# Chunked attention feeding a top-1 mixture of experts: the order in which a pair's keys, queries and values are asked for

## The chip, the cores and the metric

One core of a Trainium2 chip runs the whole program. The metric is device time in microseconds (us) of one execution, as the median of the runs shown.

## The reference, cut to what matters

```python
B, H, S, D = 4, 8, 768, 64          # batch, heads, sequence, head size
chunk, left_ctx, right_ctx = 32, 16, 8
for c in range(S // chunk):          # 24 chunks
    q_c   = q[:, :, 32*c : 32*c+32]
    k_ctx = k[:, :, max(0, 32*c-16) : min(S, 32*c+40)]     # v_ctx likewise
    scores = scale * q_c @ concat(mem_k, k_ctx).T          # 8 memory keys in front
    a = softmax(scores)
    out[:, :, 32*c : 32*c+32] = a @ concat(mem_v, v_ctx)
x = out as (3072 tokens, 512)
e = argmax(x @ w_gate + modality_bias[modality_id])        # one of 8 experts per token
y[token] = gate * (relu(x @ w1[e]) @ w2[e])                # 512 -> 1024 -> 512
```

## The kernel before, in words

The attention works on 16 **pairs** of heads, numbered u = 0 to 15 (two heads of one batch entry, 128 columns together). Each pair has two halves (hf = 0 and 1) of 12 chunks, and the main loop goes over these 32 units, written `(u, hf)`. The order on every engine is the order of the program text: nothing is rearranged by a planner, so an instruction that waits holds up all that stands behind it on its engine or queue. In the turn of one unit the loop computes the scores of that unit (`scores`, L329), the transposed exponentials of the unit before it (`trans_p`, L346), the product with the values of the unit before it (`attend`, L358), and the transpose of the normalized result of the unit before that (`trans_x`, L383). Beside it the loop prepares the next pairs.

Three kinds of transfer bring a pair's inputs in, all issued on SyncE's queue (SP):

- `load_qk(u)` (L94) asks for the keys and then the queries of pair u, one DMA each, into tiles of a pool with three buffers. The keys' buffer comes free when the keys of pair u - 3 have been transposed (`trans_k`, L311), the queries' buffer when the queries of pair u - 3 have been regrouped (`regroup_q`, L278, on VectorE).
- `load_v(u)` (L255 to L257) asks for the values of pair u with six DMAs into one of three window tiles. It has to wait until `attend` of the second half of pair u - 3 has read that tile.
- `load_mv(u)` (L264) copies the memory values into the same tile with two DMAs.

From pair 6 on the keys of pair u + 2 are half transposed in unit (u, 1) and the other half in unit (u + 1, 0), and `regroup_q(u + 2)` runs in unit (u, 1). GpSimd (POOL) spreads the values of pair u + 1 to the overlapping windows in unit (u, 1): `share_v`, two copies at L268, which wait for the values to land. Behind them on POOL stand, in order, the store of pair u - 1's result (`store_x`, L376), for some pairs a store of gates (L623), the memory keys of pair u + 2 (`mem_keys`, L303), which `scores(u + 2, 0)` needs, and for every fourth pair POOL's share of the routing's one-hot matrices (L657, L660), which the matmuls at L668 read.

After four pairs the tokens of one batch entry are complete, and `route` picks their experts in small steps between the attention's. The expert matmuls follow the attention; the weights of the first expert are asked for once three of the four batch entries have been routed.

The end of the turn of unit (u, 0), for u from 1, issues the loads: values and memory values of pair u + 2 (`NVW` is 3), then keys and queries of pair u + 4. `NU` is 16.

Of the kernel before, what the change touches and what calls it, by code (L numbers as in the profile page):

```python
# [45 lines left out]
def tile_chunk_attention_top1_moe(  # L46
# [16 lines left out]
    NU = B * H // 2  # L63
# [25 lines left out]
    def load_qk(u):  # L89
        r0 = u * 2 * S  # L90
        q2s[u] = ld.tile([P, 6, 2 * D], F32, name="q2")
        k2s[u] = ld.tile([P, 6, 2 * D], F32, name="k2")
        for t, f in ((k2s[u], kf), (q2s[u], qf)):
            nc.sync.dma_start(t.rearrange("p (h i) e -> p h (i e)", h=2), f[r0:r0 + 2 * S].rearrange("(h p j) d -> p h (j d)", h=2, p=P))  # L94
# [153 lines left out]
    def load_v(u):  # L248
        vw = vws[u % NVW]
        for h in range(2):  # L250
            hh = 2 * u + h
            r0 = 64 * h

            src = bass.AP(tensor=vf.tensor, offset=(hh * S + 8) * D, ap=[[D, 32], [32 * D, NCH - 1], [1, D]])
            nc.sync.dma_start(vw[r0 + 24:r0 + 56, h, 0:NCH - 1, 0:D], src)  # L255
            nc.sync.dma_start(vw[r0 + 24:r0 + 48, h, NCH - 1, 0:D], vf[hh * S + S - 24:hh * S + S])
            nc.sync.dma_start(vw[r0 + 16:r0 + 24, h, 0, 0:D], vf[hh * S:hh * S + 8])  # L257

    def load_mv(u):
        vw = vws[u % NVW]  # L260
        for h in range(2):
            hh = 2 * u + h
            r0 = 64 * h
            nc.sync.dma_start(vw[r0 + 56:r0 + 64, h].rearrange("p c d -> p (c d)"), mvx[hh // 16][8 * (hh % 16):8 * (hh % 16) + 8].rearrange("p c d -> p (c d)"))  # L264
# [691 lines left out]
    for i in range(n + 2):  # L956
        live = i < n
        u, hf = units[i] if live else (NU, i % 2)
# [124 lines left out]
        if i < 2:  # L1083
            load_qk(i + 3)
        if live and hf == 0 and u >= 1:
            if u - 1 + NVW < NU:
                load_v(u - 1 + NVW)
                load_mv(u - 1 + NVW)
            if u + 4 < NU:
                load_qk(u + 4)  # L1090
        if i == 5:
            small_loads()
# [251 lines left out]
```

## Time and profile before

| | |
|---|---|
| median of 3 runs | 424.61 us |
| the three runs | 423.15, 424.61 and 427.23 us |
| the profiled execution, its own time | 421.46 us |
| its span, from the first to the last instruction | 419.7 us |
| mean granted TensorE clock | 0.997 of full speed |
| TensorE busy (PE) | 402.2 us, 96% of the span |
| VectorE (DVE), ScalarE (ACT), GpSimd (POOL) busy | 338.8, 301.4 and 238.8 us |
| DMA packets | 82543, of which 50659 are under 512 bytes |

The rows below come from the profiled execution. Times are microseconds from the start of the span. The span is 1.76 us shorter than that execution's time, and that execution was 3.15 us faster than the median of the three runs. The attention takes the first 130 us or so of the span. A busy TensorE isn't TensorE at its peak, since matmuls are pipelined and their ends are modelled.

### The profile page before, as it was taken

What the parts mean: (1) busy time and instruction counts of PE and PEld (TensorE: products, weight loads), DVE (VectorE), ACT (ScalarE), POOL (GpSimd) and SP (SyncE); (2) the same over time, 40 slices, a digit from 0 to 9 for tenths busy, and PEclk for the clock granted to TensorE, in tenths of its full rate; (3) what the DMA queues carried; (4) which work ended last, traced back from release to release, by engine and by line L of the source; (5) the groups of instructions that cost most, each with busy time, mean ns of one, the idle gap of its engine ahead of it and who ended that gap; (6) DMA issues with size and microseconds to landing.
All of it is one profiled execution on the core that took longest, in us unless ns stands there. A gap on an engine that the chain in (4) does not pass through costs nothing.

```text
span 419.7 us, 11402 instructions
## 1 busy us (share of the span) xinstructions
PE 402.2 (96%) x3875; PEld 340.6 (81%) x3875; DVE 338.8 (81%) x788; ACT 301.4 (72%) x594; POOL 238.8 (57%) x320
## 2 busy tenths in 40 slices
PE   7999998998999999999999999999999999999993
PEld 4777896787867989899998888888888888888882
DVE  7889697798897889769979887788989688988750
ACT  7777886796765557467566887868778678878750
POOL 8986678778681619776753654463866076520101
PEclk9999999999999999999999999999999999999998
DMA  9899899999859600334423769969757232410101
GB/s 218 183 271 237 196 256 184 282 238 198 197 160 261 214 15 2 102 103 76 102 76 61 274 207 266 316 165 357 211 209 232 78 79 79 91 61 2 51 3 56
DMA packets 82543, 66.81 MB, mean 159 GB/s; under 512 B 50659, under 2 KB 71339, under 8 KB 82476
## 3 DMA queue, kind: packets, MB, share of 16 engines
q1 hardware_dynamic: 75276, 46.36, 44.7%
q0 software_dynamic: 6784, 19.50, 15.0%
q8 instruction: 33, 0.54, 0.6%
q14 instruction: 34, 0.28, 0.2%
q10 hardware_dynamic: 416, 0.13, 0.1%
HBM read 84.64 MB, written 12.76 MB: 232 GB/s over the span
## 4 chain that ended last, share of the span: by engine, by line
PE 63%; issue 13%; DMA 10%; POOL 6%; DVE 5%; ACT 1%; POOLq 1%; SPq 0%; ACTq 0%; DVEq 0%
PE av L843 12%; PE tr L831 11%; PE sc L843 10%; PE tr L812 9%; PE tr L815 5%; PE av L358 3%; DMA vw<-in_v_dram 3%; DMA q<-in_q_dram 2%; PE sc L329 2%; DMA k<-in_k_dram 2%; DMA out_dram<-o,ix_now 1%; PE tr L383 1%; PE tr L346 1%; PE tr L311 1%; POOL vw L268 1%
## 5 line engine op out<-in xcount | busy, mean ns | idle before, releaser
L743 DVE TENSOR_TENSOR w<-raw,w 128x512 fp32r<-128x512 f32 x96 | 68.0, 752 | 3.9 <-ACT w L742 3.6
L812 PE MATMUL tr<-xt,w 128*128 128x512 f32 x256 | 70.1, 395 | 0.0
L843 PE MATMUL av<-wh,h 128*128 128x512 f32 x192 | 61.5, 393 | 0.0
L268 POOL COPY vw<-vw 24x1472 f32<-24x1472 f32 x31 | 44.4, 1431 | 19.2 <-DMA vw<-in_v_dram 18.0
L742 ACT CAST w<-raw 128x512 fp32r<-128x512 f32 x96 | 53.9, 622 | 1.5 <-DMA raw<-in_moe_w_dram 1.5
L843 PE MATMUL sc<-wh,h 128*128 128x512 f32 x160 | 50.8, 392 | 0.0
L812 PEld LDWEIGHTS tr<-xt,w 128*128 128x128 f32 x256 | 44.3, 189 | 7.2 <-DVE wl L824 0.8
L831 PE MATMUL tr<-xt,w 128*128 128x256 f32 x384 | 48.1, 284 | 0.7 <-DVE xt L807 0.7
L831 PEld LDWEIGHTS tr<-xt,w 128*128 128x128 f32 x384 | 46.8, 191 | 2.0 <-DVE xt L807 0.9
L321 ACT COPY kbd<-tr 64x672 f32<-64x672 f32 x57 | 44.8, 786 | 3.1 <-PE tr L315 1.9
L815 PEld LDWEIGHTS tr<-xt,w 128*128 128x128 f32 x256 | 39.2, 189 | 5.4
L843 PEld LDWEIGHTS av<-wh,h 128*128 128x128 f32 x192 | 36.0, 188 | 7.5 <-issue 0.2
L848 POOL DMA_INDIRECT out_dram<-o,ix_now x22 | 25.6, 1162 | 28.7 <-ACT o L847 23.0
L815 PE MATMUL tr<-xt,w 128*128 128x256 f32 x256 | 40.7, 281 | 0.0
L821 DVE TENSOR_TENSOR hs<-tr,hs 128x256 f32<-128x256 f32 x64 | 26.8, 419 | 13.3 <-ACT hs L818 13.2
L843 PE MATMUL av<-wl,h 128*128 128x512 f32 x96 | 37.5, 390 | 0.0
L752 POOL DMA_INDIRECT xg<-gd,gx x24 | 27.8, 1156 | 14.8 <-DMA gd<-gt 9.2
L822 ACT ACTIVATE h<-hs 128x256 fp32r<-128x256 f32 x64 | 26.8, 418 | 12.0 <-DVE hs L821 10.3
L843 PEld LDWEIGHTS sc<-wh,h 128*128 128x128 f32 x160 | 30.0, 188 | 6.4 <-issue 0.2
L824 DVE TENSOR_TENSOR wl<-vw,wh 128x512 fp32r<-128x512 f32 x48 | 33.3, 694 | 2.3
L825 DVE SCALAR_TENSOR_TENSOR h<-hs,h 128x256 fp32r<-128x256 f32 x64 | 28.3, 442 | 7.7 <-ACT h L822 7.7
L752 POOL DMA_INDIRECT xg<-xd,gx x24 | 27.8, 1157 | 8.7 <-issue 4.8
(266 smaller groups left out, 902.8 us busy)
## 6 DMA issues: line engine op xcount, KB each, us to landing
raw<-in_moe_w_dram SPq DMA_DIRECT2D x96, 256.0 KB
vw<-in_moe_w_dram SPq DMA_DIRECT2D x72, 256.0 KB
k<-in_k_dram SPq DMA_DIRECT2D x16, 384.0 KB
q<-in_q_dram SPq DMA_DIRECT2D x16, 384.0 KB
xd<-xb POOLq DMA_DIRECT2D x16, 384.0 KB, 5.2
kbd<-in_moe_w_dram SPq DMA_DIRECT2D x24, 256.0 KB
vw<-in_v_dram SPq DMA_DIRECT2D x32, 184.0 KB
xall<-in_moe_w_dram SPq DMA_DIRECT2D x4, 1024.0 KB
```

What stands on the lines that cost most here:

```text
L268: copy(vw[r0:r0 + 24, h, 1:NCH, 0:D], vw[r0 + 32:r0 + 56, h, 0:NCH - 1, 0:D])
L321: copy(dst.rearrange("p c (i j) -> p c i j", j=2)[:, :, :, j], win)
L742: nc.scalar.copy(wh[i], raw[i])
L743: (eng or nc.vector).tensor_sub(wl[i], raw[i], wh[i].bitcast(F32))
L752: nc.gpsimd.indirect_dma_start(out=xg[t][:, part], out_offset=None, in_=rows, in_offset=bass.IndirectOffsetOnAxis(ap=gx[:, t:t + 1], axis=0))
L812: nc.tensor.matmul(ph, wh[f][:, c * P:(c + 1) * P], xt[:, c].rearrange("p a n -> p (a n)"), start=(c == 0), stop=False, skip_group_check=True)
L815: nc.tensor.matmul(ph[:, 0:256], wl[f][:, c * P:(c + 1) * P], xth[:, c], start=False, stop=(c == 3), skip_group_check=True)
L821: nc.vector.tensor_add(hs, ph[:, 0:256], hs)
L824: nc.vector.tensor_sub(wl[w], raw[w], wh[w].bitcast(F32))
L825: nc.vector.scalar_tensor_tensor(hl[:, f], hs, 0.0, hh[:, f].bitcast(F32), op0=ALU.max, op1=ALU.subtract)
L831: nc.tensor.matmul(ph, w[f][:, c * P:(c + 1) * P], x[:, c, :], start=(n == 0), stop=(n == 11))
L843: nc.tensor.matmul(pos[t], x, w[8 + f], start=(f == 0 and n == 0), stop=(f == 7 and n == 2))
```

## The change

```diff
         if live and hf == 0 and u >= 1:
+            if 3 <= u < NU - 4:
+                load_qk(u + 4)
             if u - 1 + NVW < NU:
                 load_v(u - 1 + NVW)
                 load_mv(u - 1 + NVW)
-            if u + 4 < NU:
+            if u < 3:
                 load_qk(u + 4)
```

In the nine turns u = 3 to 11 the two DMAs of `load_qk(u + 4)` now stand in front of the eight DMAs of `load_v(u + 2)` and `load_mv(u + 2)` on SP, where they stood behind them. The turns u = 1 and 2 keep the old order, and from u = 12 on there are no keys left to ask for. No instruction is added or taken away, and no other engine's order changes.

## Rows read from the trace of the kernel before

**Rows 1.** Busy time by stretch: us, five engines (instructions), clock, DMA share, GB/s.
```profile
50.00:60.00 10.00, 10.00 (x199) 8.93 (x198) 8.45 (x28) 8.62 (x17) 5.68 (x6) 1.00 1.04 239
```

**Rows 2.** Waits of the engines, 30 to 115 us: total, times, longest.
```profile
POOL vw L268 <- DMA vw<-in_v_dram: 17.1, 10, 3.1
...
DVE qr L278 <- DMA q<-in_q_dram: 2.5, 4, 1.6
...
PE tr L311 <- DMA k<-in_k_dram: 1.1, 1, 1.1
```

**Rows 3.** Waits of SP's queue, 40 to 110 us.
```profile
SPq L264 <- DMA q<-in_q_dram: 7.2, 7, 1.6
```

**Rows 4.** Chain that ended last, in order of time: start, length, what.
```profile
59.45 5.69 DMA vw<-in_v_dram
...
65.16 6.47 DMA k<-in_k_dram
```

**Rows 5.** PE by time: start, length, line, operation, idle time before and its releaser.
```profile
60.34 0.87 PE L358 MATMUL av<-vw,PT 128*32 128x130 f32 x24
...
63.43 0.87 PE L358 MATMUL av<-vw,PT 128*32 128x130 f32 x24
64.12 0.84 PE L329 MATMUL sc<-kbd,qT 128*32 128x128 f32 x24
...
67.17 1.23 PE L668 MATMUL tr<-a,l 128*128 128x192 f32 x6
68.33 0.88 PE L358 MATMUL av<-vw,PT 128*32 128x130 f32 x24
...
71.76 0.52 PE L311 MATMUL tr<-ident,k 128*128 128x128 f32 x3 [1.10 <-DMA k<-in_k_dram]
...
72.72 0.87 PE L358 MATMUL av<-vw,PT 128*32 128x130 f32 x24
...
75.45 0.27 PE L311 MATMUL tr<-ident,k 128*128 128x128 f32 x1 [0.51 <-issue]
...
76.48 0.87 PE L358 MATMUL av<-vw,PT 128*32 128x130 f32 x24
```

**Rows 6.** SP's queue by time: the issues around three pairs.
```profile
52.91 0.40 SPq L255 DMA_DIRECT2D vw<-in_v_dram  x1
...
58.44 0.39 SPq L94 DMA_DIRECT2D k<-in_k_dram  x1
58.94 0.40 SPq L94 DMA_DIRECT2D q<-in_q_dram  x1
59.45 0.40 SPq L255 DMA_DIRECT2D vw<-in_v_dram  x1
...
65.16 0.39 SPq L94 DMA_DIRECT2D k<-in_k_dram  x1
```

**Rows 7.** PE by time: the transpose that frees a keys' buffer.
```profile
52.66 0.49 PE L311 MATMUL tr<-ident,k 128*128 128x128 f32 x3
```

**Rows 8.** DMA issues by line, KB each.
```profile
k<-in_k_dram SPq DMA_DIRECT2D x16, 384.0 KB
q<-in_q_dram SPq DMA_DIRECT2D x16, 384.0 KB
```

**Rows 9.** Busy time by stretch, as in Rows 1, in shorter stretches.
```profile
44.00:46.00 2.00, 2.00 (x31) 1.64 (x27) 1.97 (x6) 1.95 (x4) 1.64 (x2) 1.00 0.37 47
...
60.00:62.00 2.00, 2.00 (x54) 1.64 (x53) 1.90 (x9) 1.96 (x4) 1.99 (x2) 1.00 1.00 350
62.00:64.00 2.00, 2.00 (x34) 1.83 (x36) 1.97 (x5) 1.92 (x6) 1.79 (x5) 1.00 1.33 209
66.00:69.00 3.00, 2.44 (x36) 1.83 (x38) 2.86 (x7) 2.40 (x5) 2.94 (x3) 1.00 0.66 73
```

**Rows 10.** POOL by time: values shared, memory keys, one-hot matrices.
```profile
58.54 2.88 POOL L268 COPY vw<-vw 24x1472 f32<-24x1472 f32 x2 [2.23 <-DMA vw<-in_v_dram]
...
63.06 0.73 POOL L303 COPY kbd<-memT 64x192 f32<-64x192 f32 x2
...
66.53 1.01 POOL L660 TENSOR_SCALAR a<-iota,ac,tokm 128x192 fp32r<-128x192 f32 x1
67.61 2.87 POOL L268 COPY vw<-vw 24x1472 f32<-24x1472 f32 x2
```

## The prediction

> **What bounds the kernel now.** I read the profile from coarse to fine: busy time by stretch, then who waited for whom, then the chain that ended last, then the queue and the two engines around the places that the chain names. In a stretch of the attention's middle TensorE's records cover all of the 10 us and the DMA engines' mean share is 1.04, at 239 GB/s [rows 1]. So both the attention's own work and the transfers are close to their limit, and neither has much to give. The waits say which of them is late. By far the longest is POOL's, 17.1 us in ten places, for values to land; VectorE waits 2.5 us for queries and TensorE itself only 1.1 us, once, for keys [rows 2]. The reader should not take the longest for the costliest: POOL's wait costs only where somebody waits for POOL.
>
> Where somebody does is seen in TensorE's own steps. The product with the values opens each turn's last part. From 60.34 to 63.43 two of them are 3.09 us apart, with no idle time of note between them; that is the step when nothing is late. The one at 72.72 comes 4.39 us after that at 68.33, so 1.30 us late, and the transpose at 71.76 shows why: 1.10 us of idle time, ended by keys that landed [rows 5]. These are the keys of pair 10. The chain goes through the same place: keys asked for at 65.16, 6.47 us until they were there, and their issue itself came right after values asked for at 59.45 had taken 5.69 us [rows 4]. SP doesn't run ahead freely; its issues of the memory values waited 7.2 us in seven places for queries asked for earlier [rows 3]. The queue moves at the pace at which transfers land.
>
> All other late steps that I can name (routing matmuls, VectorE and ScalarE between two of them) have nothing to do with the order of the loads. So what the change can win is small against 424.61 us: the 1.30 us, and what the queries' waits cost.
>
> **What moves, and its price.** The change adds and removes nothing. Per turn it moves two DMAs, keys and queries, past eight on the same queue; no other queue is passed. Their issues take 0.39 and 0.40 us [rows 6]; 58.44 to 59.45 is the two with what lies between, 1.01 us, and that is what SP does earlier. The data is 2 x 384 KB [rows 8], 786 thousand bytes; at the 350 GB/s of the stretch in which such transfers ran [rows 9] that is 2.25 us of all DMA engines.
>
> Since the loads form a cycle (keys and queries, values, memory values), swapping them in nine consecutive turns is one shift: in turn 3 one set of keys and queries is put in, in turns 4 to 11 the cycle is the old one with keys one pair further ahead, and at turn 12 one set is missing. So keys come about one turn earlier, and values at most one set later, once, not nine times.
>
> *The keys' side.* Pair 10's keys take the place that pair 9's had, 58.44 in place of 65.16 [rows 6]: 6.72 us earlier against a lateness of 1.30 us. Could they be held up there by their buffer? It comes free with the transpose that ends at 53.15 [rows 7], 5.3 us sooner, so the values behind them aren't held up by it either. The stretch from 66 to 69, in which DMA moved only 73 GB/s [rows 9], then meets pair 11's keys, which have a turn to spare. I count the whole 1.30 us as won. The queries of pair 10 kept VectorE idle for 1.6 us [rows 2], and the step after it, 72.72 to 76.48, is 0.67 us too long; but 0.51 us of that is idle time at 75.45 which the row puts down to "issue" [rows 5], to no landing. So 0 to 0.67 us; I take 0.2, near the rest of 0.16, because the row names another reason for most of it.
>
> *The values' side.* From turn 3 on they stand behind one set more. Upper bound: the set's 2.25 us. Lower bound: the inserted set (pair 7's) is issued near 40 us and moves in a stretch where the engines have room; from 44 to 46 they moved 47 GB/s [rows 9], which is 1.7 us of 2 unused at 350 GB/s. That leaves 0.5 us. If the stretch up to 46 has more room than that, the shift is nothing, and if the queue no longer runs dry there, even some tenths below. I take 0.5, since the row that is nearest in time to the insertion says so; the range keeps 2.25.
>
> Who pays for 0.5 us? POOL spreads pair 7's values from 58.54, having waited 2.23 us for them, and behind that stand two stores, then the memory keys of pair 8, which end at 63.79 [rows 10]. The scores of pair 8 start at 64.12 [rows 5]: 0.33 us of room, the tightest place that I found. A shift of 0.5 us makes them 0.17 us late. Behind the memory keys POOL makes one-hot matrices until 67.54 [rows 10], and the routing matmuls run from 67.17 to 68.40 [rows 5], so the last of them has been waiting on POOL already and takes the full 0.5. These are the same delay seen twice, not two: 0.3 us between them. Then the next values are spread from 67.61 with no wait of POOL's before them [rows 10], so a shift up to about that size is absorbed there.
>
> What hides the rest: the longer waits of POOL in other turns have a turn's slack behind them, and by then TensorE waits for neither. If that cover were gone, each 1 us of shift would be 1 us at most per place.
>
> The sum: -1.30 - 0.2 + 0.3 = -1.2 us. Whatever the attention wins reaches the end, because the first expert's work starts from the last pairs. Against the profiled execution's own time, 421.46 us (span 419.7), this gives 420.3; that execution was 3.15 us faster than the median of the three runs, so for the median I take 424.61 - 1.2 = 423.4 us.
>
> **A rule weighed against the trace.** After the keys' issue at 58.44 and the values' at 59.45 [rows 6] the stretch 60 to 62 runs at 350 GB/s and the stretch 62 to 64 at 209 [rows 9], as if large packets went first and small ones after. The Trainium skill, page "DMA: Bandwidth & Descriptors", section "Queues, rings and completion order", says that each DMA engine takes the descriptors of one ring in their order; by that, what is put in front delays what stands behind by its full length, and the shift would be 2.25 us. The trace agrees on the order; it doesn't say that no gap absorbs the length. What a full shift would cost is the third rival's sum, which is made from rows.
>
> **The rivals.**
>
> *Nothing comes of it (424.6 us).* The 1.30 us at 72.72 may be an accident of this execution: one wait of 1.1 us in one place, and the other queries late by 0.3 us on average (below). If the routing's POOL work is the true limit between 63 and 74, the step at 76.48 takes over and the gain of 1.5 us goes to it. For it: only one of nine turns shows a late key. Against it: the chain passes through that very key.
>
> *SP's issuing is the bound (424.6 us).* From 58.44 to 65.16 one cycle of ten issues fills 6.72 us of the queue [rows 6]. If that is the time that ten issues take, order is without effect: keys come earlier, something else comes later by as much, and every turn is as long as before. For it: hardly a gap in that cycle. Against it: SP waits for landings inside it [rows 3], so issue follows data. The Trainium skill, page "Perfetto Trace Analysis", section "What "DMA-bound" means", names a solid track of the issuing sequencer as a bound of its own, and by it this rival would hold; the trace shows the solid track, and the waits speak against the conclusion.
>
> *Values become the bound (slower: 426.2 us).* Mechanism: the set put in front in turn 3 isn't absorbed, pair 7's values land 2.25 us later, POOL's memory keys for pair 8 are late by 2.25 - 0.33 = 1.92 us, and TensorE waits at 64.12. It decides from a shift of 0.33 + 1.5 = 1.83 us on, where the loss passes the gain. Once gives -1.5 + 1.92 = +0.4; if the second routing stretch, with the same POOL work behind the same wait, pays again, 1.92 more, so +2.3, and I put the case between, at +1.6. For it: POOL's 17.1 us of waits show that values land last in most turns. Against it: the 47 GB/s just where the set goes in.
>
> *More is won (422.1 us).* If all waits on queries cost their time (2.5 us on VectorE) beside the 1.30 and nothing is paid for the values: -3.8 at most, -2.6 if half of the queries' is hidden. For it: VectorE is 85% busy [rows 1], so its idle time isn't all spare. Against it: queries' waits other than the longest average (2.5 - 1.6) / 3 = 0.3 us.
>
> That the loads don't come earlier at all (SP held at the keys' buffer) is excluded for pair 10 by the 5.3 us above.
>
> **How the numbers follow.** Forecast (between -2 and -0.4 us) 0.48, nothing 0.19, SP's issuing 0.08, slower 0.14, more 0.11. The three runs lie 4.1 us apart, so a shift under 1%, 4.2 us, can hardly be told from none with them. All five cases lie inside 1%; only their tails and the spread of the runs reach beyond. So faster 0.06, same 0.89, slower 0.05. The range takes in "more" and "slower" with about 1 us for the median's own scatter at the low end and half of that at the high end: 420.8 to 426.7 us.
>
> **What the profile after would show.** Right: the transpose of pair 10's keys without idle time for a landing, and keys asked for one turn earlier on SP; VectorE's waits for queries near nothing; POOL's waits for values as long as before or longer by half a microsecond each. The values' step is wrong if the scores after the memory keys, or the routing matmuls, show idle time ended by POOL, or if the first attention product of a pair waits for POOL's copies. The prediction as a whole fails if the attention ends more than 3 us earlier or later than before, which would mean that the order of loads decides more turns than the one that I found.

## The result, and the profile after

The median went from 423.17 us (420.98 to 427.23) to 425.93 us (423.71 to 429.78), 22 runs of each: a ratio of 1.0054 [1.0033, 1.0074], so slower by some 2.3 us (0.0054 of 423.17) where 1.2 us faster was forecast, and within 1% of before. Ratios and intervals go by fast runs alone: runs over 1.5% above the fastest of their kernel are left out, none of these 44 and, further down, one of the keys alone, two of the same with the memory keys in front and one of the last run of experiment 5. The profiled execution after has a span of 423.5 us, 3.8 more than that of before, at the same mean clock of 0.997; through the attention the granted clock was 1.00 in both.

The loss is made in the attention's middle. First TensorE by time, after, the same columns as in [rows 5]:

```profile
45.44 0.87 PE L358 MATMUL av<-vw,PT 128*32 128x130 f32 x24
...
51.27 0.86 PE L358 MATMUL av<-vw,PT 128*32 128x130 f32 x22 [0.47 <-POOL vw L268]
52.88 0.86 PE L329 MATMUL sc<-kbd,qT 128*32 128x128 f32 x24 [0.74 <-POOL kbd L303]
...
60.02 0.86 PE L329 MATMUL sc<-kbd,qT 128*32 128x128 f32 x24 [0.54 <-POOL kbd L303]
...
67.83 0.86 PE L329 MATMUL sc<-kbd,qT 128*32 128x128 f32 x24 [1.42 <-POOL kbd L303]
...
71.17 0.80 PE L668 MATMUL tr<-a,l 128*128 128x192 f32 x5 [0.76 <-POOL a L660]
71.91 0.87 PE L358 MATMUL av<-vw,PT 128*32 128x130 f32 x24
...
75.00 0.87 PE L358 MATMUL av<-vw,PT 128*32 128x130 f32 x24
...
78.21 0.27 PE L311 MATMUL tr<-ident,k 128*128 128x128 f32 x1 [0.66 <-issue]
...
121.28 0.87 PE L358 MATMUL av<-vw,PT 128*32 128x130 f32 x24
```

And the same view of before, at three points that the earlier rows don't show:

```profile
45.86 0.87 PE L358 MATMUL av<-vw,PT 128*32 128x130 f32 x24
...
51.51 0.84 PE L329 MATMUL sc<-kbd,qT 128*32 128x128 f32 x24
...
118.28 0.87 PE L358 MATMUL av<-vw,PT 128*32 128x130 f32 x24
```

Put the two side by side as "after minus before". The product with the values at 45.44 is still 0.42 us early. The scores of pair 6 are 1.37 late (52.88 against 51.51), those of pair 7 are at 60.02, and those of pair 8 are 3.71 late (67.83 against 64.12 in [rows 5]). At the next product the lateness is 3.58 (71.91 against 68.33), and then it falls to 2.28 (75.00 against 72.72): that fall of 1.30 us is the late key of [rows 5], which is gone. From there the lateness wanders to 3.00 at 121.28. So the gain came as forecast in this pair of executions, and about 4 us were lost ahead of it, 3.2 of them (0.47 + 0.74 + 0.54 + 1.42) in idle time of TensorE that POOL ended. The 0.76 us at 71.17 are POOL's too, but the lateness doesn't grow across them (3.71 ahead, 3.58 behind): the same routing matmuls were drawn out in the kernel before [rows 5].

The waits of the engines after, 30 to 118 us, columns as in [rows 2]:

```profile
POOL vw L268 <- DMA vw<-in_v_dram: 21.9, 8, 5.0
...
PEld sc L329 <- POOL kbd L303: 3.9, 4, 1.7
...
PE sc L329 <- POOL kbd L303: 2.7, 3, 1.4
...
PE tr L668 <- POOL a L660: 0.8, 1, 0.8
...
PE av L358 <- POOL vw L268: 0.5, 1, 0.5
```

The lines on keys and queries that landed late in [rows 2] have no counterpart in this list at all. New are TensorE's waits for POOL: 2.7 us for memory keys, 0.8 for one-hot matrices, 0.5 for spread values, 4.0 together against 1.1 for keys before. POOL's own wait for values went from 17.1 to 21.9 us.

Now POOL by time, after (columns as in [rows 10]), and under it the same of before:

```profile
47.97 3.25 POOL L268 COPY vw<-vw 24x1472 f32<-24x1472 f32 x2 [4.99 <-DMA vw<-in_v_dram]
51.17 0.88 POOL L376 DMA_DIRECT2D xd<-xb  x1
52.09 0.73 POOL L303 COPY kbd<-memT 64x192 f32<-64x192 f32 x2
...
67.04 0.73 POOL L303 COPY kbd<-memT 64x192 f32<-64x192 f32 x2
```

```profile
44.30 2.88 POOL L268 COPY vw<-vw 24x1472 f32<-24x1472 f32 x2 [0.98 <-DMA vw<-in_v_dram]
...
48.06 0.73 POOL L303 COPY kbd<-memT 64x192 f32<-64x192 f32 x2
```

Pair 5's values, the first that stand behind the set put in front, are spread from 47.97 in place of 44.30, 3.67 us later. The memory keys of pair 6 stand behind that on POOL and are done at 52.82 in place of 48.79. Before, that left 2.7 us until the scores at 51.51; after, the scores start 0.06 us behind them. The chain of waits of this stretch goes through the same steps, in order of time:

```profile
41.94 5.98 DMA vw<-in_v_dram
...
47.97 1.29 POOL vw L268
...
51.22 0.83 POOL xd L376
...
52.48 0.35 POOL kbd L303
...
52.88 0.86 PE sc L329 x24
```

One more execution of each kernel was profiled, with no edit, to see whether this is one execution's accident. Of before:

> The kernel before, a second profiled execution. Theory of the prediction (pair 10's keys are late by the order of the loads): TensorE waits for keys again at the same transpose, 0.7 to 1.5 us, and the step there is over 4.2 us. Rival (the 1.30 us were an accident of that one execution; the two profiled kernels in the old order that followed show no wait for keys): no wait for keys over 0.3 us, and the attention is 1 to 2 us shorter from pair 4 to pair 14 than in the first profile.

Of after:

> The changed kernel, a second profiled execution. Theory (late values through POOL): pair 5's values are spread from 47 to 49 us, scores wait for POOL's memory keys in at least three places, 2 to 4 us in all, and from pair 4 to pair 14 the attention is 2.5 to 4.5 us longer than in the second execution of the kernel before. Rival (collisions of VectorE's small steps with POOL's copies, which fall out differently each time, make the difference): scores' waits for POOL under 1 us and the excess in VectorE's long instructions at least 2 us above the kernel before.

The spans were 422.2 and 425.2 us, and the granted clock was 1.00 through the attention again. The waits of the second execution of before:

```profile
DVE qr L278 <- DMA q<-in_q_dram: 2.1, 3, 1.0
...
PE tr L311 <- DMA k<-in_k_dram: 1.7, 2, 1.2
```

and of the second one of after:

```profile
POOL vw L268 <- DMA vw<-in_v_dram: 25.4, 10, 5.0
...
PE sc L329 <- POOL kbd L303: 2.2, 2, 1.5
...
PE tr L668 <- POOL a L660: 1.3, 2, 0.8
```

Both patterns come back in these two executions: late keys and queries in the old order only, TensorE waiting for POOL's memory keys and one-hot matrices in the new one only. Their sizes don't. At pair 10's transpose the second execution of before waited 0.53 us, under the 0.7 expected, and the step there was 3.81 us, not over 4.2; its other wait for keys, 1.19 us, stands at pair 13's. Three variants further down that keep the old order (the controls of experiments 1 and 3 and the last run of experiment 5) show no wait of TensorE for keys in this stretch at all. So what the keys' side has to give differs from execution to execution. In the new order the scores waited in two places this time, where at least three were expected, and across the routing matmuls the lateness now did grow, by 0.73 us.

Pair 5's values were spread from 45.23 in the second execution of before and from 49.38 in that of after, 4.15 us apart. Over all profiles of this study with the small loads in their old place it is 44.30 to 45.69 in the five that keep the old order in this turn, and 47.83 to 49.38 in the four with the whole set in front: 3.5 us between the means, and no overlap. From the product at 45.44 (or its counterpart) to the one at 121.28 the attention took 72.42 and 72.70 us before, 75.84 and 76.10 after: 3.4 us more both times. The prediction was to count as failed if the attention ended more than 3 us later; its last product with the values starts 3.38 us later in the first pair (132.90 against 129.52) and 4.57 in the second.

### The profile page after: what moved, and what is told of

Same layout as the page of the kernel before. It is cut to its first block, busy times and chain, and to the rows that moved or that the text cites. A ratio compares the mean times of both kernels' runs of the same rounds, so it can differ in the third digit from the quotient of the medians.

```text
span 423.5 us, 11409 instructions
## 1 busy us (share of the span) xinstructions
PE 403.6 (95%) x3872; PEld 340.6 (80%) x3875; DVE 335.5 (79%) x788; ACT 300.3 (71%) x594; POOL 236.4 (56%) x320
## 4 chain that ended last, share of the span: by engine, by line
PE 46%; issue 18%; DVE 12%; POOL 11%; DMA 10%; ACT 2%; POOLq 1%; SPq 0%; ACTq 0%; DVEq 0%
PE av L843 9%; PE tr L831 8%; PE sc L843 8%; PE tr L812 6%; DMA out_dram<-o,ix_now 4%; POOL xg L752 3%; PE tr L815 3%; PE av L358 3%; PE sc L329 2%; DVE xb L371 2%; DMA gd<-gt 2%; POOL planes L777 2%; POOL vw L268 1%; DMA vw<-in_v_dram 1%; PE tr L383 1%
## 5 line engine op out<-in xcount | busy, mean ns | idle before, releaser
L743 DVE TENSOR_TENSOR w<-raw,w 128x512 fp32r<-128x512 f32 x96 | 64.8, 719 | 3.8 <-ACT w L742 3.6
L268 POOL COPY vw<-vw 24x1472 f32<-24x1472 f32 x31 | 44.5, 1437 | 23.3 <-DMA vw<-in_v_dram 21.9
L825 DVE SCALAR_TENSOR_TENSOR h<-hs,h 128x256 fp32r<-128x256 f32 x64 | 27.3, 426 | 7.7 <-ACT h L822 7.3
L818 ACT COPY hs<-tr 128x256 f32<-128x256 f32 x64 | 23.6, 369 | 12.9 <-PE tr L815 9.9
```

The lines of the kernel that those rows point to most:

```text
L268: copy(vw[r0:r0 + 24, h, 1:NCH, 0:D], vw[r0 + 32:r0 + 56, h, 0:NCH - 1, 0:D])
L743: (eng or nc.vector).tensor_sub(wl[i], raw[i], wh[i].bitcast(F32))
L825: nc.vector.scalar_tensor_tensor(hl[:, f], hs, 0.0, hh[:, f].bitcast(F32), op0=ALU.max, op1=ALU.subtract)
```

## The experiments

The theory after this reading: the set put in front delays the values by some 4 us, POOL stands still for them, and what stands behind them on POOL (memory keys, which the scores need; one-hot matrices, which the routing matmuls need) makes TensorE wait. The rivals: that the loss comes from crowded transfers as such; that the small loads which the set meets (L171 to L174, on SP just in front of it) make the shift so long; that a swap which begins later, or a smaller set, would cost nothing.

Each run is compared with runs of the kernel before on the same chip. Ratios are to those, with the 95% interval.

**1. Memory keys in front of the spreading.** The kernel after, with `mem_keys(u + 2)` of pairs 6 to 14 moved on POOL from behind the values' spreading to in front of it:

```diff
         if AHEAD <= u < NU - 1 and hf == 0:
-            if u < NU - 2:
-                mem_keys(u + 1, nc.gpsimd)
...
+            if AHEAD - 1 <= u < NU - 3:
+                mem_keys(u + 2, nc.gpsimd)
             if u == NU - 2:
                 share(u + 1, 0, nc.gpsimd.tensor_copy)
             else:
                 share_v(u + 1)
```

> The changed kernel, with POOL's memory keys of pairs 6 to 14 moved half a turn earlier, in front of the spreading of the values before them, so that the scores no longer stand behind a wait for values. The loads keep the changed order. Theory (late values cost through the memory keys behind them on POOL): the scores' waits for POOL, 3.9 us in four places in the changed kernel, go; what stays is the attention products' wait for the spread values, under 1 us, and the pair-10 keys' 1.3 us is won: 1 us faster to 0.5 us slower than before, ratio 0.997 to 1.001. Rival (the later values cost by themselves, through transfers that are late, and POOL's order is without weight): the loss of 2.3 us stays, ratio 1.004 to 1.007.

Measured 1.0031 [1.0001, 1.006], above the theory's range and below its rival's. The scores wait for POOL nowhere any more. POOL by time and then TensorE by time in this kernel:

```profile
57.25 0.96 POOL L303 COPY kbd<-memT 64x192 f32<-64x192 f32 x2
61.44 2.88 POOL L268 COPY vw<-vw 24x1472 f32<-24x1472 f32 x2 [3.23 <-DMA vw<-in_v_dram]
```

```profile
64.86 0.27 PE L329 MATMUL sc<-kbd,qT 128*32 128x128 f32 x1
...
69.36 0.80 PE L668 MATMUL tr<-a,l 128*128 128x192 f32 x5 [1.22 <-POOL a L660]
...
87.05 0.52 PE L346 MATMUL tr<-ident,sb 128*128 128x128 f32 x3 [1.19 <-DVE den L366]
```

Pair 8's memory keys are done at 58.21 and its scores begin at 64.86, with 6.6 us of room. But the values are as late as in the kernel after (pair 5's were spread from 47.83), and the routing matmuls wait 1.22 us for the one-hot matrices that still stand behind them on POOL. At 87.05 TensorE waits 1.19 us more, for VectorE: a small routing step there (L555) took 1.42 us at 83.55 in place of 0.21, beside POOL's copies of values, which began at 83.50. So one way from the late values to TensorE is closed, and others are open.

The control is the same move in the kernel before:

> The kernel before, old order of the loads, with POOL's memory keys of pairs 6 to 14 half a turn earlier, as in the run that had them in the changed kernel. Theory (they cost only where values are late enough; in the kernel before no scores wait for POOL): within 0.3% of before, ratio 0.997 to 1.003. Rival (the earlier memory keys are of use by themselves, and hid the loss of the changed order rather than removed it): about as much faster as the changed kernel gained by it, ratio 0.996 to 0.998.

1.0005 [0.9975, 1.0036]. With the old order of loads the move is worth nothing, so what it gave above isn't a gain of its own.

**2. From which turn.** The swap only from the turn of pair 6 on (shown against the kernel after):

```diff
-            if 3 <= u < NU - 4:
+            if 6 <= u < NU - 4:
                 load_qk(u + 4)
...
-            if u < 3:
+            if u < 6:
                 load_qk(u + 4)
```

> The new order starts in turn 6 (keys of pair 10) and not in turn 3. Theory (the set of keys and queries put in front in turn 3 delays pair 5's values by 3.7 us and every later pair's with them; POOL's memory keys stand behind those values, and the scores of pairs 6 to 9 wait for them): the set now goes in front of pair 8's values, which POOL could not spread before 67.6 us anyway because of its routing work, so most of the delay is covered there; pair 10's keys still come early and the 1.3 us at 72.7 are won. Expected 0.3 to 2 us faster than before, ratio 0.995 to 0.999, no scores of pairs 6 and 7 waiting for POOL. Rival 1 (keys in front cost in every turn in which they stand there): six of nine turns remain, so about two thirds of the 2.3 us loss, ratio 1.003 to 1.005. Rival 2 (only the meeting with the small loads of turn 2 costs): same as the theory here, told apart by the run with the small loads moved.

1.0033 [1.0006, 1.0059], where I had expected a gain; it lies in the range of the first rival. The scores of pair 8 are no longer late, but those of pairs 9 and 12 are; TensorE by time:

```profile
75.82 0.86 PE L329 MATMUL sc<-kbd,qT 128*32 128x128 f32 x24 [0.79 <-POOL kbd L303]
...
97.92 0.86 PE L329 MATMUL sc<-kbd,qT 128*32 128x128 f32 x24 [1.25 <-POOL kbd L303]
```

The loss moved to where the shift now begins, and beyond. Neither of the two beginnings tried has room for it. With the memory keys in front as well:

> The new order from turn 6 on, with POOL's memory keys of pairs 6 to 14 half a turn earlier. The run from turn 6 without that lost 0.33% and showed 2.0 us of scores waiting for POOL at pairs 9 and 12. Theory: these two waits go, what is left are the routing's matmuls waiting for POOL's one-hot matrices (1.2 us there), so at most half of the loss stays: ratio 0.998 to 1.002. Rival (the order in which memory keys stand has no part in the loss): ratio 1.002 to 1.006.

1.0016 [0.9981, 1.005], and again no wait of the scores for POOL.

The opposite, the swap in the turn of pair 3 alone (`if u == 3:`, the old order in all others), so that one set is put in and the order is mended one turn later:

> The new order in turn 3 alone; from turn 4 on the old one, so that pair 6's values and all later ones stand behind the same sets as before. Theory (one shift, which every later turn inherits as long as the order stays): pair 5's values land late as in the changed kernel and scores of pair 6 wait for POOL, about 1.4 us; the values of pairs 6 to 8 land as before or at most 1 us later, so the further loss at pairs 7 and 8 (another 2 us) doesn't come; the keys of pair 10 are late again, 1.3 us. Expected 0.5 to 2 us slower than before, ratio 1.001 to 1.005, with scores waiting for POOL in one or two places, not four. Rival (the whole loss is made in turn 3 and only carried on): scores wait for POOL in four places as in the changed kernel, and with the late keys beside it the loss is above 2.3 us, ratio 1.006 to 1.009.

1.0047 [1.0014, 1.008]. POOL by time:

```profile
48.55 2.87 POOL L268 COPY vw<-vw 24x1472 f32<-24x1472 f32 x2 [4.92 <-DMA vw<-in_v_dram]
...
53.10 2.88 POOL L268 COPY vw<-vw 24x1472 f32<-24x1472 f32 x2
```

The first spreading is as late as with the whole change, the second waits for nothing: the shift is over after one turn. As the theory had it, the scores wait for POOL in one place and not in four (0.75 us, at 53.09), and pair 10's keys are late again (0.53). But time is lost elsewhere as well: 0.53 us at the routing matmuls, for POOL, and 0.92 at the transposes of L346, for VectorE. TensorE's records nearly fill this stretch before [rows 1], so I take it that a microsecond lost in one place isn't made up later.

**3. The small loads.** `small_loads()` stands on SP just in front of the set. Moved behind it, to unit 7 (`i` counts the units), with `gate_weights()` (and the bias rows beside it) from unit 8 to unit 9:

```diff
-        if i == 8:
+        if i == 9:
             gate_weights()
...
-        if i == 5:
+        if i == 7:
             small_loads()
```

> The changed kernel, with the four small loads (gate weights, modality, biases) asked for one pair later, behind pair 5's values, and POOL's two steps that read the gate weights one unit later. Theory (the set's own 2.25 us and its cold start are the delay): pair 5's values still land 2 to 3 us later than before, and the loss of 2.3 us shrinks by at most a third, ratio 1.003 to 1.006. Rival (the set meets the many tiny packets of the small loads, which the changed profile's chain names with 3.85 us): without them in front pair 5's values land within 1 us of before and the loss goes, ratio 0.997 to 1.001.

1.0115 [1.0065, 1.0166]. Pair 5's values were spread from 45.51, only 1.2 us later than before. But the routing's first matmuls then waited for the gate's weights; the waits of this kernel:

```profile
PE tr L531 <- POOL wg L236: 3.3, 1, 3.3
```

That is a loss of the experiment's own, so its ratio says nothing of the change. Its timeline is worth more, but the small loads stand in front of these values in the kernel before too. With them out of the way there as well (the control below) the values were spread from 43.56, so the set alone made 1.95 us, by one execution of each. Moved the other way, to unit 3, where they are through before the set comes:

```diff
-        if i == 5:
+        if i == 3:
             small_loads()
```

> The changed kernel with the four small loads asked for one pair earlier (behind the loads of turn 1), so that nothing that the routing needs comes later. Rival, now favoured (the set put in front in turn 3 is so slow because it meets the small loads' tiny packets; with them later pair 5's values were spread from 45.5 us and not from 48.0): pair 5's values are spread from 44.5 to 46 us, the scores of pair 6 don't wait for POOL, and most of the loss goes: ratio 0.999 to 1.003. Theory (the set's own length): spread from 46.5 to 48 us, scores of pairs 6 to 8 wait for POOL, ratio 1.004 to 1.007.

1.0082 [1.005, 1.0113]. Both expectations are missed. In its profiled execution, the longest of its runs (428.65 us against a median of 425.38), pair 5's values were spread only from 51.28, and yet the scores waited for POOL by just 0.2 us: TensorE had already waited 2.4 us for keys and VectorE 3.5 us for queries. That execution was late before the new order could act: the keys of pair 5 were asked for at 31.14, in the control's at 27.86, and up to there the two programs are the same. After the wait for keys (TensorE busy for 0.33 of the 2 us from 42) the granted clock was 0.50, the lower of its two levels (1.2 and 2.4 GHz), from 44 to 50. So this profile doesn't show the usual way in which this kernel loses. The control, the same move in the kernel before:

> The kernel before with the same move of the small loads alone: the control for the run above. If the small loads cost nothing where they were, within 0.3% of before, ratio 0.997 to 1.003. If they held up loads there too, up to 1 us faster, ratio 0.996 to 1.000; pair 10's keys are late as before or by less.

1.0000 [0.9967, 1.0032] (by medians it was faster, 421.56 against 423.18 us, so a small gain isn't excluded). The rival that small loads alone make the loss falls: where they don't stand beside the set, it is no smaller.

**4. Half the set.** Keys in front of the values, queries still behind (the second argument, new in `load_qk`, picks keys, 0, or queries, 1):

```diff
             if 3 <= u < NU - 4:
-                load_qk(u + 4)
+                load_qk(u + 4, (0,))
...
             if u < 3:
                 load_qk(u + 4)
+            elif u + 4 < NU:
+                load_qk(u + 4, (1,))
```

> Half of the change: in turns 3 to 11 the keys alone go in front of the values, the queries stay behind them. One shift of 384 KB and not 768. Theory (the delay of the values is the length of what is put in front, and costs from some 2.7 us of it on, the room of pair 6's memory keys): pair 5's values are spread from 45.5 to 46.5 us (44.3 before, 48.0 in the changed kernel), the scores of pair 6 hardly wait, and pair 10's keys are early: ratio 0.998 to 1.003. Rival (any new order in front of pair 5's values costs the same, by a start of the queue that runs dry): as the changed kernel, ratio 1.004 to 1.007.

1.0067 [1.0031, 1.0104]: the values of pair 5 came at 46.59, nearly as a smaller shift should have it, and yet nothing was won over the whole set: the time lies in the rival's range. The profiled execution, at 423.62 us, was faster than its kernel's median of 425.83, and its scores hardly waited for POOL, so a second one was profiled:

> The half change (keys alone in front) once more, for its profile: its timed loss of 0.67% is larger than the 1.1 us that its first profile showed between pairs 4 and 14. If that profile was a lucky one, scores and routing matmuls wait for POOL by 2 us or more here and pairs 4 to 14 take 2 to 4 us longer than in the kernel before. If not, the loss of the half change lies outside the waits for POOL.

Its waits (this kernel's lines are 3 further down):

```profile
PEld sc L332 <- POOL kbd L306: 4.0, 4, 2.1
DVE qr L281 <- DMA q<-in_q_dram: 3.3, 3, 1.8
...
PE sc L332 <- POOL kbd L306: 3.1, 2, 1.8
...
PE tr L671 <- POOL a L663: 1.5, 2, 0.8
```

From the product at 46.12 to the counterpart of the one at 121.28 it took 76.05 us, so the first profile was the lucky one. It loses in the same places as the change, with the late queries of the old order on top. The memory keys in front, added to this:

> The half change with POOL's memory keys half a turn earlier. Theory (late values cost through the memory keys): at least half of the 0.67% goes, ratio 0.999 to 1.0035. Rival (the half change loses elsewhere): ratio 1.004 to 1.008.

1.0019 [0.9982, 1.0056], with no wait of the scores for POOL.

**5. Both moves together.** Memory keys in front and small loads in unit 3, once in the new order of loads and once in the old:

```diff
+            if AHEAD - 1 <= u < NU - 3:
+                mem_keys(u + 2, nc.gpsimd)
...
-        if i == 5:
+        if i == 3:
             small_loads()
```

> The changed kernel with both moves, memory keys half a turn earlier and small loads one pair earlier. Theory (late values cost through POOL's memory keys, and the small loads only add to the lateness): below the changed kernel with the small loads earlier alone (1.0082) by at least 0.3%, ratio 1.000 to 1.005. Rival (the small loads in front of turn 2's loads cost by themselves in the new order): ratio 1.006 to 1.009.

1.0047 [1.0019, 1.0075], as the theory had it.

> The old order of the loads with both moves that were neutral alone: POOL's memory keys half a turn earlier and the small loads one pair earlier. If values and keys are both on time in the old order once nothing small stands in their way, the waits for keys that two profiles of the kernel before showed (1.1 and 1.7 us) go and no scores wait for POOL: 0.2 to 0.6% faster than before, ratio 0.994 to 0.998. If those waits are covered by something else that is late next, no change, ratio 0.998 to 1.002.

0.9985 [0.9955, 1.0014]: the lowest ratio of the study, and not to be told from the kernel before. Its profile shows no wait for keys, and the gain hoped for from that doesn't show.

One rival stands beside all these runs: the clock. In the profiles of four variants TensorE's granted clock fell from 1.00 to the lower level for some microseconds, each time behind a stretch of 2 us in which TensorE had been busy for 0.00 to 0.81 us: with the small loads later (0.50 from 52 to 54 us), with them earlier (0.50 from 44 to 50), with the keys alone and the memory keys in front (0.53 and 0.62 in the two stretches from 70 to 74), and with both moves in the new order (0.50 from 74 to 76). In the second of these the 24 matmuls of a product with the values then took 1.53 us in place of 0.87. So what a wait costs there isn't the wait alone. It doesn't make the differences of the table below, though: the mean granted clock of all runs is 0.9957 over the four new orders without the move and 0.9955 with it, and 0.996 in the kernels before and after.

Since single intervals overlap, the pairs are read together. Each row is one order of loads without and with the memory keys in front:

| order of loads | without | with |
|---|---|---|
| the change | 1.0054 | 1.0031 |
| from pair 6 on | 1.0033 | 1.0016 |
| keys alone | 1.0067 | 1.0019 |
| the change, small loads in unit 3 | 1.0082 | 1.0047 |
| old order | 1 | 1.0005 |
| old order, small loads in unit 3 | 1.0000 | 0.9985 |

Over the four new orders the mean loss is 5.9 per mille without the move and 2.8 with it, a difference of 3.1; adding the half widths of the eight intervals in squares gives 2.2 for it. So the move takes away about half, some 1.3 us, by these ratios. The plain means of all runs, none left out, give less: 5.1 and 3.2, a difference of 1.9 with much the same uncertainty. In the two old orders the move changes the ratio by +0.5 and -1.5 per mille, so no gain of the move by itself is seen there.

## Why the prediction was wrong

The measured median, 425.93 us, lies inside the range that I gave (420.8 to 426.7), by the range's width alone: a change 1.2 us faster was forecast and one 2.3 us slower came.

**What bounds the kernel** was read rightly: transfers at the pace at which they land, the attention's own work with no time to give, POOL's waits that cost only where somebody waits for POOL.

**The keys' side** held in its mechanism. The 1.30 us at 72.72 were won, the waits for keys and queries are gone in two executions of the kernel after and there in two of that before. That it was 1.30 us is the luck of the first execution: 0.53 stood in that place in the second, and none in three variants with the old order, as the rival "Nothing comes of it" had suspected. The 0.51 us at 75.45 that I had left out as "issue" is still there (0.66 at 78.21), so it belonged to no landing, and the step around it is no shorter (4.24 us from 75.00, against 3.76 from 72.72): the 0.2 us for queries weren't seen. The keys of pair 10 were asked for at 62.23, not at 58.44 as I had said: the queue was itself later by then, and it was early enough. SP's queue after:

```profile
40.07 0.41 SPq L94 DMA_DIRECT2D k<-in_k_dram  x1
...
41.94 0.41 SPq L255 DMA_DIRECT2D vw<-in_v_dram  x1
...
62.23 0.40 SPq L94 DMA_DIRECT2D k<-in_k_dram  x1
```

**The values' side** is the step that failed, and in it first the size: "I take 0.5, since the row that is nearest in time to the insertion says so". It was 3.67 us (4.15 in the second pair of executions), beyond my upper bound of 2.25. The row of 47 GB/s from 44 to 46 [rows 9] is right, and lies on the wrong side: pair 5's values, the first behind the set, had landed by 44.30 in the kernel before. The idle room stood behind the transfer that was to be delayed, and what is put in front of a transfer can use only room ahead of it. The stretches after:

```profile
42.00:44.00 2.00, 2.00 (x54) 1.63 (x54) 0.73 (x4) 1.96 (x5) 0.91 (x3) 1.00 0.93 277
44.00:46.00 2.00, 2.00 (x34) 1.83 (x36) 1.55 (x6) 1.95 (x4) 0.00 (x0) 1.00 1.16 220
```

The engines now work through to 46, at a DMA share of 0.93 and 1.16, but at 277 and 220 GB/s and not at the 350 by which I had turned the set's bytes into 2.25 us. At such rates 786 thousand bytes take 2.8 to 3.6 us. The shift has two parts: the values were asked for 1.96 us later (41.94 against 39.98 before), and took 5.98 us to land where they had taken 4.3 (39.98 to 44.30). The Trainium skill, page "DMA: Bandwidth & Descriptors", section "Queues, rings and completion order", has each engine take the descriptors of a ring in their order; my working had that rule beside it and set it aside for the idle room. The 2.25 us that I had worked out by it were nearer than the row that I chose, and the measured delay went beyond them as well. With the small loads out of the way in both orders (experiment 3) the shift was 1.95 us, with half the set 2.3 and 2.6 (46.59 against 44.30, and 46.91 in the second execution). How the 3.7 us divide between bytes and small packets isn't settled, since each of these runs changed other times too.

In it second, who pays. I had found pair 8, with 0.33 us of room, and wrote of the rest that "the longer waits of POOL in other turns have a turn's slack behind them". I had measured that in one turn only. Pair 6's memory keys had 2.7 us, much room against 0.5 and too little against 3.67. And I had counted one shift as one payment. TensorE paid 0.47 and 0.74 us at the values of pair 5 and the memory keys of pair 6, 0.54 at pair 7 and 1.42 at pair 8: several payments, each smaller than the shift, that together (3.2 us) come near its size. I had also let the routing pay once for the delay; its 0.76 us added nothing in this pair of executions, and 0.73 in the second.

**The rival "Values become the bound"** is what happened. Its mechanism, memory keys behind late values, is shown by the waits and by what the move in experiment 1 takes away; its case that the routing pays again is seen in some executions (1.22 us of waiting in experiment 1) and not in others. Its sum, +1.6 us, was near the 2.3 measured partly by luck: it was put between +0.4 and +2.3 by choice (their middle is 1.35), and its shift of 2.25 met one kind of tight place where a longer one met several. Its chance was too low: the 0.14 hung on the 47 GB/s.

The other rivals: "Nothing comes of it" and "More is won" fall with the loss. "SP's issuing is the bound" would have left the time as it was.

Shown: the late values, POOL's stand-still, the waits behind it, and that a part of the loss, about half by the ratios, goes through the memory keys. The rest, 2.8 per mille (1.6 of uncertainty by the same sum over four intervals) or some 1.2 us, is argued from the traces. All four kernels with a new order and the memory keys in front show the same wait between 87 and 93 us: TensorE stands still before the transposes of L346, until VectorE is done, for 1.19 (experiment 1), 1.82 (from pair 6 on), 1.20 (keys alone) and 1.06 us (small loads in unit 3). In each of them the routing step L555 ahead of it took 1.42 to 1.44 us in place of 0.21, while POOL copied values. In the kernel after that wait is 0.50 and 0.85 us, and in the five profiles with the old order throughout there is none at this place. So the changed times of POOL's copies, by which they meet VectorE's routing steps, are the likeliest rest, with the routing's waits of 1.5 and 1.2 us for POOL in two of the four and the lower clock in two. Since no kernel moved these steps or the one-hot matrices out of the way of the copies, how the rest divides stays open.

## What to carry to other kernels

Before idle transfer time is counted as cover for a load put in front, look whether it lies ahead of the transfer that is pushed back; room behind it covered nothing here. When a shift is passed on from turn to turn, write down the room at every place that inherits it, and count each payment until the sum reaches the shift. And on an in-order engine the price of a late load is set by what stands behind the wait: moving that work in front of the wait (the memory keys here) took away about half of the price here, and was worth nothing that could be measured while the load wasn't late. A wait of about 1 us in one profile needs a second profile before a forecast rests on it.

## What the runs showed of the hardware

I hadn't expected small VectorE operations to stretch beside POOL's copies. VectorE by time in the kernel after, then POOL:

```profile
86.50 1.38 DVE L555 SCALAR_TENSOR_TENSOR eq<-l,rev 128x48 f32<-128x48 f32 x1
```

```profile
84.94 2.88 POOL L268 COPY vw<-vw 24x1472 f32<-24x1472 f32 x2 [1.72 <-DMA vw<-in_v_dram]
```

The same operation took 0.21 us at 53.56, where POOL wasn't copying. Here it ends 0.06 us after the copies. The regrouping of queries did the same in the kernel before: 1.71 us at 87.45, inside the copies from 87.34 to 90.44, against 0.56 at 50.12. The Trainium skill, page "SBUF — State Buffer", section "Who interferes with whom", says that VectorE operations with two inputs in SBUF, and copies in a two-port mode, share a port pair with GpSimd and that the later one waits for the whole instruction; these two rows agree with that. It has a part in the loss: at 89.32 the transposes of L346, whose input VectorE makes behind this step, had waited 0.50 us for VectorE, and in the variants named above up to 1.82. How large the part is isn't known, since it falls out differently in each execution; in the second one of after L555 took 0.21 us, another step behind it (L561) 0.74, and the wait was 0.85.
